# A band of eight heads, whole weight rows, earlier state-model loads and a new order in a two-branch attention and state-space kernel

## The chip, the cores and the metric

The kernel runs on one core of a Trainium2 chip. TensorE does the matrix products into PSUM, VectorE (DVE), ScalarE (ACT) and GpSimd (POOL) work on SBUF and, but for GpSimd, on PSUM; SyncE (SP) issues nearly all DMAs. Each engine takes its instructions in order and waits on semaphores. The metric is the device time of one execution in microseconds. Three runs of the kernel before gave a median of 142.18 us (141.98 to 142.41).

## What is computed

Two branches read 2,048 tokens of width 448 each, in bf16; their outputs stand side by side in an output of 2,048 x 896.

```python
# A: attention, H = 16 heads of Dh = 28, window W = 8 with a dilation of 2
qkv = x @ wqkv                       # 448 x 1344
idx = pos[:, None] - arange(8) * 2   # a token sees itself and 7 earlier ones, two apart
logits = einsum("bhsd,bhswd->bhsw", q, kg) * Dh**-0.5   # masked where idx < 0
o = einsum("bhsw,bhswd->bhsd", softmax(logits), vg)
a = o.reshape(B, S, D) @ wo
# B: a diagonal complex state model with 448 states
h = Lam_bar * h + Bu[:, t, :]        # over 2,048 steps
y = 2.0 * einsum("blp,dp->bld", hseq, Cmat).real + x * Dskip
```

## The kernel before

One function defines some 60 small steps (`@op`), and a string, `ORDER` (L31 to L59), lists 556 calls of them. A loop at the end (L808) runs through the list and emits each step's instructions, so the list sets the order on every engine. A token is a step's name, its indices, after `@` the PSUM banks that it uses, and for an eviction from PSUM the engine: `.` is ScalarE, `=` VectorE. Capital names (`QK`, `AV`, `C`) are mostly TensorE steps, the small ones (`qk`, `av`, `c`) their evictions. The loads that stand ahead of the list (L138 to L162) are issued first.

Branch A. x is loaded token-major into `xbuf`; its first 1,024 tokens are transposed on TensorE (`XA`, `XH`, evicted by `xa`, `xh`), the second 1,024 by four DMA transposes into `xT` (L157). `wqkv` is loaded by `w_load` (rows 0 to 383, as three tiles of 128) and `w_half` (the last 64 rows, twice, into the lower and the upper partitions); before the change the columns of q and k come in pieces of 256 and 192. GpSimd copies the last 64 columns of q and k together into `wq6` (L211). `QS` and `QK` make q and k, head dimension on partitions (`part`, L231), `V_` makes v token-major, also through L231. `P` multiplies q by eight shifted k on VectorE (L346), `E_` sums over each head's 28 rows by a matmul with a 0/1 matrix (L358, L362), four column tiles of 32 side by side. `lt`, `TR`, `tr` scale and transpose the logits, `sma`, `smb`, `smc` are the softmax, into `attn`, for a token 8 weights by 16 heads.

The weighted sum over a token's window is a banded matrix product, and the band is built by DMA. `AL` shifts the weights to the key's token by a matmul with a shifted identity (L426, L429) and `al` evicts them into a row of zeros, `Ak`: for one key token and one tile of tokens, 128 weights (8 places by 16 heads) and then zeros up to 640. `ad` writes the rows to a DRAM buffer `pd`; `sp` reads it back with a row pitch that is 16 elements short (L444, four DMAs per call, 32 partitions each), so that each key token's weights land 16 elements further right than the one's before: `PT` holds, for every key token (partition), the weights of 135 query tokens, 16 heads side by side. `AV` (L470, L475) multiplies v of a head (32 columns) by this band; the moving operand takes every 16th element, `4 * hg + hh:H * n:H`. One call has 16 such matmuls, in four groups of four heads, each head in its own 32 columns of the array; calls with B = 1 have four more of 7 columns. There are eight calls for each half of the tokens (B = 0, B = 1), two of a tile pair's four head groups and two parities. `av` evicts, `W_` multiplies by `wo` (L488), `w` evicts and `ow` stores.

Branch B. x is loaded a second time, regrouped, into `xnB` (`LX`, twelve DMAs, L616) and transposed by four DMAs into `xbuf` (`xt`, L644); `Bn` (L162) is transposed into `BT` (`BD`, L620), C into `Cw` (`CD`). `BU` is the input product (L231), `BR`, `UP`, `DN`, `H_` are rotations that carry the state within four steps and between halves, `sa`, `sb`, `sd` the scan on VectorE, `cs` and `ca` scale C, `C` is the output product (L755), `c` adds x times Dskip (`xd`) and `oc` stores.

SP takes its DMAs in the order of the program text and of the list: the loads, `BD`, `xt`, `LC`, `XR`, `CD`, `wo`, then `ad` and `sp`, then the stores.

Of the kernel before, what the change touches and what calls it, by code (L numbers as in the profile page):

```python
# [9 lines left out]
BF16 = mybir.dt.bfloat16  # L10
# [11 lines left out]
PW = H * (128 + 7)  # L22
# [9 lines left out]
WU@0 XA00@0 XA01@1 xa00= XH0@2 xa01. PP@3 xh0. pcopy pa QS00@4 pb pd_ pc XH1@5 XA11@6 pe xh1. XA10@7 ty0 QS10@0  # L32
xa11. xa10= qk000. QK061@13 tf0 qk010. QK021@25 QS01@6 ty5 P000 ts00 QK041@74 QS11@0 tf5 QK040 pf P001 qk001. QK060
qk011. pg ts10 ts05 qk041. QK020 ts20 ts15 qk040. V_100@60 P010 qh001. ty1 qk021. V_010@47 rb1 ts25 qh000. tf1 V_011
qk020. V_101 QK031@51 qh011. rb0 QK030 v100. ty2 P011 v101. QK050@26 LX qk031. tf2 qk030. ts01 V_001@01 P020 QK051
ts11 V_000 qk050. qk051. P021 qh010. V_110@52 v011. rb3 ts21 QK140@63 v000. P030 ty4 v010. ts02 QK120@70 v001. tf4
hc0 rb2 ts12 V_111 ts04 QK141 E_00@41 v110. v111. E_01 P031 qk141. E_02 qk140. QK101@52 QK121 ts22 P040 QK100 qk120.
qk121. P041 ts14 BD V_510@36 ty3 ts24 qk100. P050 V_511 ty6 V_501@70 V_500 v511. tf6 P051 xt0 QK110@56 ts06 ts16
v510. tf3 v500. QK111 E_03 P060 qk110. E_04 v501. E_05 xt2 qk101. P061 V_410@37 ts03 ts13 P100 qk111. E_06 ts26 ts23
V_411 P101 QK131@50 lt00 QK161@26 xt3 QK130 lt01 v410. P110 v411. TR0@4 qk131. P111 QK150@13 qk130. tr0. xt1 P120  # L40
V_401@70 QK151 QK160 qk151. P121 qk150. E_10@54 P130 qh110. LC E_11 qh101. V_400 qh100. P131 qh111. E_12 sma0 v401.
E_13 hc1 v400. XR BU301@31 BU401@26 BU001@07 BU400 P140 smb0 P141 BU300 P150 OZ z40. BU000 z30. ci1= ci2. BR31 ci3=
BR41 CD1 BU200@23 z00. P151 z31. ci0. BR01 P160 CD3 BU310@01 z41. z01. P161 BU311 CD2 BU501@67 BU201 E_14 smc0 E_15
CD0 E_16 BR32 lt11 BU500 lt10 z20. TR1@4 z32. BR21 z50. BU100@52 tr1= z21. sma1 BR51 BU211@06 z51. BU101 BU210 z10.
OP pm3 xd2 smb1 pm0 wo BR11 BU011@43 z11. smc1 BU111@75 BR22 BU010 z22. ca3 AL0@2 BR23 BR02 al0. BR33 BU110 pm1 z02.
ad0 z23. xd1 z33. ca1 BR03 BR12 AL1@0 cs3 BU410@24 al1= z12. xd3 z03. ad1 BR13 UP3 sp0 UP0 pm4 z13. BU411 cs1 y0.
BU601@07 UP1 y3. BR42 UP2 y1. BU600 ca2 sa0 pm2 AL2@3 z42. sp1 BU510@15 z60. sb0 y2. ca6 BU511 BU611@20 sd0 BR43
BR52 BR61 z43. BU610 al2. z61. cs2 ad2 z52. DN1@6 AL3@3 dn1 BR53 DN0@7 al3. UP4 H_21@1 dn0 BR62 z53. H_11@6 h21 ad3
y4. H_01@3 z62. H_10@7 h11 UP5 H_20@4 H_00@1 y5. BR63 h20 ca4 AV030@2 sp2 sa2 AV020@6 AV010@5 av030. AV031@4 av020.
cs4 AV000@2 av010. AV021@6 av031. sb2 AV011@5 av000. AV001@4 av011. cs6 W_30@2 av021. sp3 h01 av001. W_10@5 sd2 z63.  # L50
w30. W_20@6 w10. ow30 ca5 UP6 W_00@3 w20= ow10 h10 W_31@4 ow20 y6. w00. DN3@2 DN2@5 W_11@6 ca0 dn2 ow00 dn3 W_21@7
sa4 W_01@0 w11. w21. ow11 H_12@3 H_22@5 w01. w31= ow21 H_13@2 AV121@6 sb4 ow01 ow31 AV110@7 av121. AV120@0 h12 h13
AV100@4 av120. sd4 AV131@6 av110. av100. AV130@3 av131. AV101@2 av130. sa6 AV111@0 av101. DN4@7 h22 DN5@4 av111.
W_70@6 dn4 W_40@3 dn5 w70. cs5 H_02@2 ow70 W_50@0 sb6 h00 W_61@5 w50. sd6 w40. H_14@7 ow50 W_71@4 w61. ow40 cs0
H_03@6 ow61 W_51@1 h03 W_60@0 w51. w71. DN6@3 W_41@5 dn6 ow71 h14 H_15@6 H_26@1 w41. w60= H_25@4 H_24@3 ow41 H_23@7
h25 C32@5 ow60 h23 ow51 h26 H_04@0 H_05@4 h24 C31@7 xd0 C33@1 h05 h15 C23@3 c33 c32 oc33 H_06@4 oc32 C30@6 c23 h06
oc23 H_16@1 C20@5 h16 h04 C22@3 c31 oc31 C21@4 c22 c30 oc22 h02 C12@1 oc30 c20 C11@0 oc20 c12 c21 oc12 C13@7 oc21
c11 oc11 C03@3 C10@6 c03 c13 oc03 C02@2 oc13 C01@5 c02 c10 oc02 C00@1 oc10 c01 oc01 c00 oc00
# [3 lines left out]
def kernel(  # L62
# [64 lines left out]
    def w_load(c, n, *at):  # L127

        for d in at:
            SP.dma_start(wq[:, 0:3, c + d:c + d + n], wq_r[:, :, c + d:c + d + n])  # L130

    def w_half(s, c, n, *at):

        o, i = (bass.AP(t.tensor, t.offset + c + at[0], [list(t.ap[0]), [D, len(at)], [1, n]])
                for t in (wq[64 * s:64 * s + 64, 3], A_wqkv[384:448]))
        SP.dma_start(o, i)  # L136
# [3 lines left out]
    w_load(0, 256, 0, D)  # L140
    w_half(0, 0, 256, 0, D)
    SP.dma_start(xnA[:, 4:8], xA_r[:, 4:8])
    w_half(1, 0, 256, 0, D)
    w_load(256, 192, 0, D)
    for s in range(2):
        w_half(s, 256, 192, 0, D)
    w_load(0, D, 2 * D)
    for s in range(2):
        w_half(s, 0, D, 2 * D)

    xA1 = xbuf[:, 8 * D:].rearrange("p (t n) -> p t n", n=2 * D)
    for d0, d1, b, c in ((0, D, 8, 0), (D, 512, 12, 384), (512, 896, 12, 0)):
        SP.dma_start(xA1[:, :, d0:d1], xA_r[:, b:b + 4, c:c + d1 - d0])

# [5 lines left out]
    for ri, b in enumerate((B_B_re, B_B_im)):  # L160
        for d0, d1, c in ((0, D, 0), (D, 512, 384)):
            SP.dma_start(Bn[64 * ri:64 * ri + 64, :, d0:d1], b[:, c:D].rearrange("(g p) d -> p g d", p=64))  # L162


    xnB = keep.tile([128, 4, T, D], BF16, tag="xnB")
    xP = xnB.rearrange("p c j d -> p c (j d)").rearrange("p c (a n) -> p c a n", a=2)
    xB_r = B_x[0].rearrange("(q p h a b) d -> h p q a b d", q=2, p=128, h=2, a=2)
# [249 lines left out]
    @op  # L417
    def AL(g):
        p = pp["al", g] = ps()
        p4 = p.rearrange("p (t w h) -> p t w h", t=4, w=W)  # L420

        def at(t0, n, cc):
            return attn[:, t0:t0 + n, cc:cc + H]
        for w in range(W):
            cc = 32 * (3 - w // 2) + 16 * (w % 2)
            PE.matmul(p4[:, :, w, :], shf[:, 135 + w:263 + w], at(4 * g, 4, cc), start=(w == 0), stop=True, skip_group_check=True)  # L426
            if w > 0:
                n = 4 if g < 3 else 2
                PE.matmul(p4[:, 0:n, w, :], shf[:, 7 + w:135 + w], at(4 * g + 2, n, cc), start=False, stop=True,  # L429
                          skip_group_check=True)  # L430

    @op
    def al(g, e):
        evict(e, late["Ak"][g].rearrange("p (s n) -> p s n", n=640)[:, :, 0:128], pp.pop(("al", g)).rearrange("p (s n) -> p s n", n=128))
# [5 lines left out]
    @op  # L440
    def sp(g):
        sl = (4 * g) % NS
        for s in range(4):
            SP.dma_start(late["PT"][32 * s:32 * s + 32, sl:sl + 4, 512 * s:512 * s + 624],  # L444
                         pd_ap(g, 32 * s * 2560, [[2560 - H, 32], [640, 4], [1, 624]]))
# [17 lines left out]
    @op  # L463
    def AV(B, hg, par):
        PT = late["PT"]
        p = pp["av", B, hg, par] = ps()
        if B > 0:
            for hh in range(4):
                PE.matmul(p[32 * hh:32 * hh + 32, 0:7], v_s[:, 8 * B - 2 + par, 4 * hg + hh, :],
                          PT[:, 6 + par, 128 * H + 4 * hg + hh:PW:H], start=True, stop=True, skip_group_check=True)  # L470
        for bl in range(4):
            t = 8 * B + 2 * bl + par
            n = 135 if bl < 3 else 128
            for hh in range(4):
                PE.matmul(p[32 * hh:32 * hh + 32, 128 * bl:128 * bl + n], v_s[:, t, 4 * hg + hh, :],  # L475
                          PT[:, t % NS, 4 * hg + hh:H * n:H], start=(bl == 0 and B == 0), stop=True, skip_group_check=True)
# [133 lines left out]

    @op
    def LX():
        for hh in range(2):
            for d0, d1, b, c in ((0, D, 0, 0), (D, 512, 1, 384), (512, 896, 1, 0)):
                for q in range(2):
                    SP.dma_start(xP[:, 2 * hh + q, :, d0:d1], xB_r[hh, :, q, :, b, c:c + d1 - d0])  # L616
# [164 lines left out]
    @op  # L781
    def OP():
        cl.close()
        s6 = pool("a_pt")
        for n, shape in (("oT", (2, 4, 2, 512)), ("PT", (NS, PW)), ("wo", (4, D)), ("ya", (6, D))):
            late[n] = s6.tile([128, *shape], BF16, tag=n, name=n)

        late["Ak"] = [Ak0[:, 0], Ak0[:, 1], late["oT"][:, 1].rearrange("p a b n -> p (a b n)")[:, 0:2560],
                      late["ya"].rearrange("p k n -> p (k n)")[:, 0:2560]]
        late["n"] = 0  # L790

    @op
    def pm(i):
# [3 lines left out]
        elif i == 3:  # L797
            POOL.memset(late["wo"].rearrange("p a n -> p (a n)").bitcast(F32), 0.0)
        else:
            POOL.memset(late["PT"][:, 4 * i:4 * i + 4].rearrange("p t n -> p (t n)").bitcast(F32), 0.0)  # L800
# [42 lines left out]
```

## Time and profile before

| what | us |
|---|---|
| median of three runs | 142.18 |
| the profiled execution | 141.91 |
| its span, first to last instruction | 140.2 |
| TensorE busy | 133.6 |
| VectorE busy | 111.7 |
| ScalarE busy | 91.4 |
| GpSimd busy | 22.7 |

The costliest TensorE groups are L231 (input products of both branches), L755, L475, L488 and L358. In a group's row the numbers after the bar are the busy time in us, the mean length of one instruction in ns, and the idle time of the engine before them. Matmuls are pipelined: one that lasts 421 ns does not keep the next from starting, so what one costs is read from the chain or from the distance between starts, not from its length. A row of the chain has its start, its length and its work; a window has its bounds and length, the busy time of each engine, the granted clock, the DMA engines' share and what they moved in GB/s.

### The profile page before, as it was taken

The page shows a single profiled execution, that of the slowest core. Times are in us where ns is not written, and L with a number is a line of the kernel's source. Part 1 is how long each engine was busy: PE and PEld are TensorE (multiplying, and loading weights), DVE is VectorE, ACT ScalarE, POOL GpSimd, SP SyncE. Part 2 cuts the span into 40 slices and gives each one's busy share as a digit, 9 for nine tenths or more (in the row PEclk, how much of TensorE's full clock was granted, in tenths as well). Part 3 has the DMA queues.
Part 4 walks back from the last instruction along what each step waited for, and adds up shares of the span by engine and source line. Part 5 has one row for each costly group of instructions (what it writes and reads, how often), then busy time and mean ns, then how long its engine had stood idle before and what let it go on. Part 6 is the DMA issues. An engine that isn't in the chain of part 4 may idle for free.

```text
span 140.2 us, 2881 instructions
## 1 busy us (share of the span) xinstructions
PE 133.6 (95%) x1074; PEld 64.0 (46%) x1083; DVE 111.7 (80%) x201; ACT 91.4 (65%) x186; POOL 22.7 (16%) x39
## 2 busy tenths in 40 slices
PE   6988999999999999999999999999999999999990
PEld 6742443433434334343455445554554555555540
DVE  0178999999899999988998989628975889777351
ACT  4279999999999899467999996599274430000000
POOL 6709000000000000049995000000000000000000
PEclk9999999999999999999999999999999999999999
DMA  4999389999999989981049996183400421214232
GB/s 126 246 267 245 91 164 189 190 312 221 165 224 209 222 184 351 271 191 34 0 188 308 227 379 167 38 202 111 133 7 0 131 81 54 98 33 153 73 101 65
DMA packets 38116, 22.62 MB, mean 161 GB/s; under 512 B 22935, under 2 KB 37079, under 8 KB 38103
## 3 DMA queue, kind: packets, MB, share of 16 engines
q1 hardware_dynamic: 38040, 22.45, 64.2%
q8 instruction: 8, 0.13, 0.4%
q14 instruction: 5, 0.04, 0.1%
q10 hardware_dynamic: 63, 0.01, 0.0%
HBM read 11.68 MB, written 6.29 MB: 128 GB/s over the span
## 4 chain that ended last, share of the span: by engine, by line
PE 89%; SPq 4%; DMA 3%; issue 1%; POOL 0%; DVE 0%; POOLq 0%
PE ps L231 38%; PE ps L755 15%; PE ps L475 11%; PE ps L488 9%; PE ps L358 4%; PE ps L670 3%; PE ps L736 3%; DMA wq<-in_A_wqkv_dram 3%; SPq L130 1%; SPq L136 1%; PE ps L315 1%; PE ps L362 1%; PE ps L426 1%; PE ps L376 1%; PE ps L723 1%
## 5 line engine op out<-in xcount | busy, mean ns | idle before, releaser
L346 DVE TENSOR_TENSOR pr<-qf,kf 128x2048 bf16<-128x2048 bf16 x24 | 28.2, 1218 | 0.3 <-ACT kf L112 0.3
L231 PE MATMUL ps<-xbuf,BT 128*128 128x512 bf16 (+1 forms) x110 | 23.9, 380 | 0.4 <-issue 0.3
L755 PE MATMUL ps<-Cw,Z 128*128 128x448 bf16 x112 | 21.8, 352 | 0.0
L231 PE MATMUL ps<-xT,wq 128*128 128x512 bf16 (+1 forms) x92 | 20.8, 380 | 0.9 <-POOL wq L211 0.5
L112 ACT CAST Z<-ps 128x512 bf16<-128x512 f32 (+1 forms) x35 | 16.1, 513 | 1.6 <-PE ps L670 1.2
L475 PE MATMUL ps<-PT,v_s 128*32 128x135 bf16 (+1 forms) x256 | 16.0, 419 | 0.0
L755 PEld LDWEIGHTS <-Z 128*128 128x128 bf16 x112 | 10.9, 98 | 10.4
L231 PEld LDWEIGHTS <-BT 128*128 128x128 bf16 (+1 forms) x112 | 8.8, 97 | 12.2 <-issue 3.4
L761 DVE TENSOR_TENSOR xbuf<-ps,xnB 128x448 bf16<-128x448 f32 x16 | 9.5, 620 | 6.0 <-PE ps L755 5.9
L741 DVE TENSOR_TENSOR Z<-ps,Z 128x512 bf16<-128x512 f32 x21 | 13.6, 680 | 0.7 <-PE ps L736 0.7
L112 ACT CAST oT<-ps 128x512 bf16<-128x512 f32 x17 | 9.6, 587 | 7.0 <-PE ps L475 7.0
L488 PE MATMUL ps<-wo,oT 128*128 128x448 bf16 x64 | 13.3, 353 | 0.0
L231 PEld LDWEIGHTS <-wq 128*128 128x128 bf16 (+1 forms) x96 | 7.7, 97 | 10.9 <-issue 2.5
L231 PE MATMUL ps<-wq,xT 128*128 128x448 bf16 (+1 forms) x64 | 12.5, 355 | 0.0
L800 POOL MEMSET PT<- 128x4320 f32 x3 | 11.0, 3699 | 2.0 <-ACT Z L112 2.0
L475 PEld LDWEIGHTS <-v_s 128*32 128x32 bf16 x256 | 7.4, 113 | 6.3 <-issue 0.4
L112 ACT CAST ya<-ps 128x448 bf16<-128x448 f32 (+1 forms) x14 | 7.0, 540 | 4.1 <-PE ps L488 1.9
L632 ACT ACTIVATE ctmp<-Cw,c2t 64x448 f32<-64x448 bf16 x14 | 9.3, 667 | 0.3
L488 PEld LDWEIGHTS <-oT 128*128 128x128 bf16 x64 | 6.2, 98 | 5.7 <-ACT oT L112 0.5
L231 PEld LDWEIGHTS <-xT 128*128 128x128 bf16 (+1 forms) x64 | 5.0, 97 | 7.8 <-issue 4.0
L112 ACT CAST v_s<-ps 128x448 bf16<-128x448 f32 x16 | 8.2, 533 | 0.1
L112 ACT CAST qf<-ps 128x512 bf16<-128x512 f32 x12 | 6.9, 595 | 0.0
(146 smaller groups left out, 184.7 us busy)
## 6 DMA issues: line engine op xcount, KB each, us to landing
PT<-pd SPq DMA_DIRECT2D x16, 156.0 KB, 3.5
xnB<-in_B_x_dram SPq DMA_DIRECT2D x2, 896.0 KB
out_dram<-ya SPq DMA_DIRECT2D x16, 112.0 KB, 1.9
out_dram<-xbuf SPq DMA_DIRECT2D x16, 112.0 KB, 1.7
pd<-Ak SPq DMA_DIRECT2D x2, 640.0 KB, 3.4
xbuf<-in_A_x_dram SPq DMA_DIRECT2D x2, 448.0 KB
xnB<-in_B_x_dram SPq DMA_DIRECT2D x4, 224.0 KB, 5.6
xnB<-in_B_x_dram SPq DMA_DIRECT2D x4, 192.0 KB, 4.0
```

What stands on the lines that cost most here:

```text
L112: (ACT.copy if e == "A" else V.tensor_copy)(o, i)
L231: PE.matmul(o, l, r, start=(first and i == 0), stop=(not first and i == len(pairs) - 1 and not more[s]))
L346: V.tensor_tensor(t[:], q.unsqueeze(1).to_broadcast((128, 4, 512)), k4, ALU.mult)
L358: PE.matmul(acc[s][32 * i:32 * i + 32], E[:, f, ws, :], t[:, i, :], start=(f == 0 and ws == 0), stop=False)
L475: PE.matmul(p[32 * hh:32 * hh + 32, 128 * bl:128 * bl + n], v_s[:, t, 4 * hg + hh, :], PT[:, t % NS, 4 * hg + hh:H * n:H], start=(bl == 0 ...
L488: PE.matmul(p[:, 0:D], late["oT"][:, b // 4, hg, par, 128 * (b % 4):128 * (b % 4) + 128], late["wo"][:, hg, :], start=(hg == 0), stop=(hg ...
L632: ACT.activation(t[a:a + 64, 0:D], Cw[b:b + 64, g, :], ACTF.Copy, scale=c2t[a:a + 64, g:g + 1])
L670: PE.matmul(pp["z", g, j][:], rot(g, 0), late["Z"][:, g, j - 1, :], start=False, stop=True)
L741: V.tensor_tensor(zz, pp.pop(("h", j, g))[:], zz, ALU.add)
L755: PE.matmul(p[:, 0:D], z, Cw[:, g, :], start=(g == 0), stop=(g == G - 1))
L761: V.tensor_tensor(yo, pp.pop(("c", j, ct))[:, 0:D], xnB[:, ct, j, :], ALU.add)
L800: POOL.memset(late["PT"][:, 4 * i:4 * i + 4].rearrange("p t n -> p (t n)").bitcast(F32), 0.0)
```

## The change

Four things change.

1. The band holds eight heads side by side (`HS = 8`) in two groups, not 16 in one. `AL` writes its places in runs of 8, `al` evicts eight pieces of 64 instead of four of 128, a row of `Ak` has eight pieces of 320 with 64 weights each, `sp` reads with a pitch 8 short, runs of 312 elements (624 bytes) instead of 624 elements, twice as many, and `AV` takes every 8th element. Sizes in bytes stay.
2. The q and k columns of `wqkv` are loaded as one piece of 896 columns.
3. The first six of the twelve loads of `xnB` are issued ahead of the four transposes of x, the other six after `Bn`, whose four loads are issued in another order; the step `LX` is gone.
4. The list is ordered anew. It has the same steps but `LX`. The evictions `xa00`, `ci3`, `al1`, `w20`, `w31` and `w60` go from VectorE to ScalarE, `xa01`, `xh0` and `w51` the other way.

```diff
+HS = 8
-PW = H * (128 + 7)
+PW = HS * (128 + 7)
...
-WU@0 XA00@0 XA01@1 xa00= XH0@2 xa01. PP@3 xh0. pcopy pa QS00@4 pb pd_ pc XH1@5 XA11@6 pe xh1. XA10@7 ty0 QS10@0
-xa11. xa10= qk000. QK061@13 tf0 qk010. QK021@25 QS01@6 ty5 P000 ts00 QK041@74 QS11@0 tf5 QK040 pf P001 qk001. QK060
...
+WU@0 XA00@0 XA01@1 xa00. PP@2 XH0@3 pcopy xa01= pa xh0= pb QS10@4 pd_ pc pe XA11@5 ty0 XA10@6 qk010. XH1@7 xa11.
+xa10= QS00@2 xh1. tf0 ty5 V_011@01 QK021@34 qk000. QS11@5 tf5 pf P000 QS01@6 QK041@72 QK020 P001 ts00 qk011. ts05 pg
...
+z62. H_00@5 H_01@0 ca4 H_21@3 h00 H_11@7 BR63 h21 AV011@4 h11 AV000@5 al3. sa2 AV031@3 av011. ad3 z63. AV020@7 sp2
+av000. AV001@1 y5. av020. AV010@4 sb2 av001. AV030@5 av010. AV021@6 cs4 av030. H_20@7 av031. UP6 sd2 sp3 H_10@1
+W_20@4 y6. W_10@5 w20. av021. h20 W_30@3 ow20 ca0 DN2@2 W_21@4 dn2 sa4 DN3@6 W_11@7 w21. w10. H_22@2 ow21 w30.
+W_00@4 dn3 ca5 ow30 h10 W_01@5 cs0 W_31@3 w00. cs5 w01. H_13@6 ow00 H_02@1 sb4 w31. AV100@4 ow01 w11. ow31 AV110@5
+av100. ow11 sd4 AV131@3 ow10 av110. AV121@7 av131. AV101@4 sa6 AV111@5 av101. h22 AV130@3 av121. h13 av111. AV120@4
+av130. sb6 H_03@2 av120. DN4@7 W_41@5 dn4 sd6 W_60@6 w41. H_23@3 ow41 H_14@4 w60. W_50@7 h23 ow60 h03 DN5@5 W_71@6
...
-    w_load(0, 256, 0, D)
-    w_half(0, 0, 256, 0, D)
+    w_load(0, 2 * D)
+    w_half(0, 0, 2 * D)
     SP.dma_start(xnA[:, 4:8], xA_r[:, 4:8])
-    w_half(1, 0, 256, 0, D)
-    w_load(256, 192, 0, D)
+    w_half(1, 0, 2 * D)
+    w_load(2 * D, D)
     for s in range(2):
-        w_half(s, 256, 192, 0, D)
-    w_load(0, D, 2 * D)
-    for s in range(2):
-        w_half(s, 0, D, 2 * D)
+        w_half(s, 2 * D, D)
...
+    def x_load(hh):
+        for d0, d1, b, c in ((0, D, 0, 0), (D, 512, 1, 384), (512, 896, 1, 0)):
+            for q in range(2):
+                SP.dma_start(xP[:, 2 * hh + q, :, d0:d1], xB_r[hh, :, q, :, b, c:c + d1 - d0])
+
+    x_load(0)
+
     xT = s2.tile([128, 2, 7, 512], BF16, tag="xT")
     for t in range(4):
         SP.dma_start(xT[:, 1, :, 128 * t:128 * t + 128], xA1[:, t], transpose=True)
...
-    for ri, b in enumerate((B_B_re, B_B_im)):
-        for d0, d1, c in ((0, D, 0), (D, 512, 384)):
+    for d0, d1, c in ((0, D, 0), (D, 512, 384)):
+        for ri, b in enumerate((B_B_re, B_B_im)):
             SP.dma_start(Bn[64 * ri:64 * ri + 64, :, d0:d1], b[:, c:D].rearrange("(g p) d -> p g d", p=64))
+    x_load(1)
...
-        p4 = p.rearrange("p (t w h) -> p t w h", t=4, w=W)
+        p4 = p.rearrange("p (t g w h) -> p t g w h", t=4, g=H // HS, w=W)
...
-            SP.dma_start(late["PT"][32 * s:32 * s + 32, sl:sl + 4, 512 * s:512 * s + 624],
-                         pd_ap(g, 32 * s * 2560, [[2560 - H, 32], [640, 4], [1, 624]]))
+            SP.dma_start(late["PT"][32 * s:32 * s + 32, sl:sl + 4, :, 32 * HS * s:32 * HS * s + 39 * HS].rearrange("p t g n -> p (t g) n"),
+                         pd_ap(g, 32 * s * 2560, [[2560 - HS, 32], [40 * HS, 64 // HS], [1, 39 * HS]]))
...
                 PE.matmul(p[32 * hh:32 * hh + 32, 128 * bl:128 * bl + n], v_s[:, t, 4 * hg + hh, :],
-                          PT[:, t % NS, 4 * hg + hh:H * n:H], start=(bl == 0 and B == 0), stop=True, skip_group_check=True)
+                          PT[:, t % NS, (4 * hg + hh) // HS, (4 * hg + hh) % HS:HS * n:HS], start=(bl == 0 and B == 0), stop=True, skip_group_check=True)
```

## The prediction

> **What bounds the kernel now.** I read the page's busy shares first, then the chain of waits, then the groups by form, and last the windows and the timeline around the places that the diff touches.
>
> ```profile
> PE 133.6 (95%) x1074; PEld 64.0 (46%) x1083; DVE 111.7 (80%) x201; ACT 91.4 (65%) x186; POOL 22.7 (16%) x39
> PE 89%; SPq 4%; DMA 3%; issue 1%; POOL 0%; DVE 0%; POOLq 0%
> ```
>
> TensorE is the bound, and the granted clock is 0.999, so no throttle hides in it. The chain in order of time enters TensorE at 11.25 us and leaves it at 136.66 us for one last addition; between, "issue" is a few times 0.05 to 0.16 us. A gain must therefore be less streaming time on TensorE, or a shorter start.
>
> ```profile
> 46.90 0.98 PE ps L358 x16
> 83.30 7.85 PE ps L475 x124
> 101.41 0.97 PE ps L475 x14
> ```
>
> These chain pieces carry the forecast. L358 (the logit sums) and L475 (attention times values, AV) both put four matmuls of 32 columns side by side in the array. Sixteen L358 matmuls stream 512 columns each in 0.98 us: 0.245 us per group of four, 0.48 ns per column. Sixteen L475 matmuls stream only 135 (or 128) columns and take the same: 7.85 us for eight operations, 0.245 us per group, 1.81 ns per column. The visible difference is the moving operand: L358 reads neighbours (2 bytes apart), L475 reads every 16th element of the band (32 bytes apart).
>
> ```profile
> L475 PE MATMUL ps<-PT,v_s 128*32 128x135 bf16 x192 | 14.7, 421 | 0.0
> L358 PE MATMUL ps<-pr,E 128*32 128x512 bf16 x96 | 6.1, 381 | 0.0
> 83.20:106.30 23.10, 23.10 (x328) 11.99 (x327) 16.74 (x36) 15.85 (x29) 0.00 (x0) 1.00 0.40 115
> ```
>
> A single L475 matmul lasts longer than an L358 one with a quarter of its columns. The last line is the window of both AV phases (length, then busy time of PE, PEld, DVE, ACT, POOL, clock, DMA share, GB/s): TensorE 23.1 of 23.1 us, VectorE 16.7, ScalarE 15.9. Those two limit what a faster AV can give.
>
> The start, from the timeline and two windows:
>
> ```profile
> 6.91 0.82 PE L315 MATMUL ps<-xT,wq 128*128 128x512 bf16 x2
> 8.55 0.41 PE L284 MATMUL ps<-ident,xbuf 128*64 128x128 bf16 x4 [0.50 <-DMA xbuf<-in_A_x_dram]
> 11.25 0.39 PE L231 MATMUL ps<-xT,wq 64*128 64x512 bf16 x2 [0.55 <-POOL wq L211]
> ...
> 4.20:6.50 2.30, 2.15 (x24) 1.75 (x22) 0.69 (x1) 0.44 (x1) 1.97 (x7) 1.00 0.86 225
> 53.00:57.00 4.00, 4.00 (x20) 1.82 (x19) 4.00 (x6) 3.90 (x8) 0.00 (x0) 1.00 1.07 381
> ```
>
> TensorE waits 0.5 us for x and 0.55 us for GpSimd's copy of the weights. Weights in 512-byte runs arrive at 225 GB/s; rows of 3,584 bytes later at 381.
>
> **The change part by part.** The profiled execution took 141.91 us (span 140.2 and 1.7 around it); the median of the three runs is 142.18, 0.27 more, added at the end.
>
> *Band of eight heads.* AV reads every 8th element, 16 bytes apart, half the step. No row shows that step. Ends: no change (1.81 ns), and L358's 0.48 ns, which makes a group 0.065 us and over 64 groups (16 operations by 4) saves 11.5 us. A loss I exclude for this part: the matmul covers half the bytes. A straight line between the two rows gives 1.10 ns, 0.149 us a group, 6.2 us saved; a time in proportion to the step gives 0.123 us and 7.8 us saved. I take 7.0, nearer to the 32-byte row than to the neighbours' row.
>
> The Trainium skill, SBUF — State Buffer, Specifications (TRN2), speaks against this: SBUF lines are 16 bytes, and full bandwidth needs at least two accesses per line. At 16 bytes, as at 32, every element opens its own line, so by that rule the step saves nothing and the time is the second case below; the trace agrees that 32 bytes are slow (1.81 against 0.48 ns) and shows no step of 16.
>
> What is late next: both AV phases, with the W, H and DN steps between, are 23.2 us of TensorE in the new order and would be 16.2. Counted from the new list by the rows, VectorE has there five h (0.68), four sa or sd of 1.69, one sa of 1.16, scans of 1.35, 1.35 and 0.68, three cs (0.675) and two dn (0.42): 17.6 us by single durations, 16.3 with the overlap that the page shows (111.7 busy where the single durations sum to 120). ScalarE has fifteen av (0.587), eight w (0.54), two ca and four more: 17.5, or 15.8 back to back (three oT evictions took 1.58 us). So the stretch ends with these engines, not TensorE: 16.3 plus about 0.9 of handing over, 17.2, since the early W steps need all four of their av, which queue on ScalarE behind al3 and z63. Saved: 23.2 - 17.2 = 6.0 us. Bounds: 6.9 (stretch 16.3) and 4.0 (stretch 19.2).
>
> AL has the same matmuls in runs of 8; its 15 take 0.43 us, 29 ns each, as short as any group here, so zero, and at most 60 x 27 = 1.6 us if each took a transpose's 56 ns. The al eviction keeps its elements: zero (v_s in runs of 28 takes 0.533 us for 448, Z in runs of 512 takes 0.600 for 512). Zeroing covers the same bytes. The band's reload keeps its bytes, with runs of 624 instead of 1,248: four DMAs per sp, issue 0.43 us against 0.47 for a 256-run x load, so 0.2 per sp on SP. At 76 to 80 us the bus moved 227 GB/s in 1,248-byte runs, 512-byte runs made 225: zero, and a rival below. The first AV comes 0.3 us sooner after AL1 in the new list (10.9 against 11.2 by the rows); sp1's last issue ended at 78.1 and the longest landing is 4.6, so at 82.7 at the latest against 83.2: slack 0.5 covers it; +0.1.
>
> *Whole rows of wqkv.* QS10 waits for 803 KB (896 columns of 448 rows) behind the first x tiles (used from 4.59), instead of 458 KB. At 225 GB/s from 4.2 that is 7.8 us; at 381, 6.3. TensorE is free at 6.9. The next x tiles (459 KB at 299 GB/s, the rate of 6.5 to 8.5 us) follow at 7.8 to 9.3, then 1.02 us of transposes and QS00 0.97: 10.0 (both before and QS10 done at 7.9) to 11.3, with the V weights there by 11.5. The kernel before has the same steps done at 11.25. So -1.2 to +0.2, middle -0.5; VectorE and ScalarE are busy 37.2 and 37.6 of the next 38.7 us, so I keep -0.2. GpSimd's copy waits for two of these loads as before, but QK060, its first reader, now comes some 7 us of TensorE work after V_011: that wait (0.55 us, inside the 11.25 above) goes.
>
> *x ahead of the transposes.* Six issues (0.47 to 0.8 us) move in front of the four transposes on SP, where SP waited 4.2 us for x: issue hidden. Their 917 KB are not: at 256 to 381 GB/s, 2.4 to 3.6 us on the bus ahead of the transposes, whose last was issued at 19.4 and landed 3.1 later, at 22.5: now 24.9 to 26.1. Their first reader, QK121, is 14.4 us of TensorE work after V_011 (10.9 to 11.5), at 25.3 to 25.9: a wait of 0 to 0.8 us. I take +0.1, because the x that they transpose also comes sooner. BD (5.13 us of issue) and xt behind it move 3 us forward: nothing, BU starts at 50. Bn's halves change places: nothing.
>
> *Order and engines.* Six evictions go from VectorE to ScalarE, three back (0.6 us each): hidden, VectorE is the closer of the two to TensorE.
>
> **Sum**: 141.91 - 6.0 - 0.2 + 0.1 + 0.1 = 135.9, and with the 0.27: **136.2 us**. Its own range: 134.6 (stretch 16.3, start -1.0) to 138.4 (stretch 19.2).
>
> **The rivals.** *The step does not matter* (AV stays at 0.98 us per operation). For it: each element is fetched alone at either step, and four streams at 1.81 ns are one fetch per 0.45 ns, near the 0.48 ns per column of a full stream, as if one element per cycle were shared by four. Against: L358's four streams do not share. Then 142.18 - 0.2 + 0.2 = 142.2, from 141.2 (start -1.0) to 143.6 (start +0.2, transposes +0.8, first AV +0.4). More of it lies above than below: the start's gain is shared with two busy engines, the waits are not.
>
> *The band's DMAs go by runs, not bytes* (the other side). Place: AV011, which needs sp0 and sp1, eight DMAs of 160 KB, 0.70 us each at 227 GB/s. If twice the runs take twice the time: 8 x 0.70 = 5.6 us late, less the slack of 0.2: 5.4. Without an AV gain that gives 147.6, at half the price 144.9. It decides as soon as the delay passes what AV saves (6.0), or the slack where AV saves nothing. Against: 225 GB/s in 512-byte runs.
>
> *Half a gain*: 1.4 ns per column saves 0.056 x 64 = 3.6 us, below the other engines' limit: 138.6.
>
> **How the numbers follow.** Forecast 0.45; half a gain 0.05; step without effect 0.38 (faster 0.06, same 0.10, slower 0.22); by runs 0.12, all slower. Faster 0.56, same 0.10, slower 0.34, where 0.3% (0.43 us) is about what can be told from no change here. The range for 8 in 10 takes the forecast's low end and the second case's high end: 134.6 to 143.6.
>
> **What would show it.** Eight AV of the first phase in 4 to 5 us instead of 7.85, L475 near 300 ns each, VectorE or ScalarE above 90% from the first AV to the last, W steps waiting for oT. If the step does nothing: L475 stays at 420 ns. If runs count: idle before the first L475, released by PT. At the start: QS10 at 6.9 to 7.8, QS00 done by 11.3. A PE wait for xT near 25 us would make the x load wrong. The prediction is wrong above all if the read step is not what slows L475.

## The result and the profile after

The changed kernel takes 144.47 us (median, 144.31 to 144.57) against 142.08 beside it: ratio 1.0164, 95% interval 1.0143 to 1.0185. It is 2.4 us slower; 136.2 was predicted. Its profiled execution took 144.46 us, span 142.7. Some comparisons below state a ratio rather than two medians, because an execution whose clock was disturbed is left out of the ratio.

The page of the changed kernel: busy shares, the granted clock in 40 slices, the chain by engine.

```profile
PE 135.0 (95%) x1083; PEld 65.2 (46%) x1083; DVE 110.3 (77%) x198; ACT 93.9 (66%) x189; POOL 22.7 (16%) x39
PEclk9965999999999999999999999999999999999997
PE 90%; DMA 5%; SPq 1%; DVE 0%; issue 0%
```

TensorE is still the bound, with 1.4 us more to do than before, not less. One digit row is new: the clock falls in the third and fourth slice. And DMA holds 5% of the chain where it held 3%.

The chain in order of time, the two groups that the forecast rested on, and the window of both AV phases:

```profile
2.99 7.60 DMA xbuf<-in_A_x_dram
10.63 1.46 PE ps L272 x12
...
85.22 7.75 PE ps L478 x122
```

```profile
L478 PE MATMUL ps<-PT,v_s 128*32 128x135 bf16 x192 | 14.8, 417 | 0.0
L360 PE MATMUL ps<-pr,E 128*32 128x512 bf16 x96 | 6.1, 381 | 0.0
85.20:108.60 23.40, 23.40 (x330) 13.05 (x330) 17.07 (x36) 16.93 (x34) 0.00 (x0) 1.00 0.51 139
```

L478 is the old L475. With half the step it takes the same: eight AV in 7.75 us (7.85 before), 417 ns each (421). The window of both phases is full of TensorE, 23.4 of 23.4 us. So the whole term that the forecast was made of, 6.0 us, is missing, and on top of that something costs 2.4 us. That is at the start (timeline of TensorE, then windows of all engines):

```profile
8.30 1.46 PE L317 MATMUL ps<-xT,wq 128*128 128x512 bf16 x3 [2.26 <-DMA wq<-in_A_wqkv_dram]
10.63 1.46 PE L272 MATMUL ps<-ident,xbuf 128*128 128x128 bf16 x12 [0.33 <-DMA xbuf<-in_A_x_dram]
```

```profile
8.30:10.60 2.30, 2.00 (x4) 0.38 (x4) 0.07 (x1) 0.27 (x1) 0.00 (x0) 0.50 1.12 274
10.60:12.60 2.00, 1.97 (x17) 1.61 (x17) 0.47 (x1) 0.90 (x2) 1.37 (x2) 0.50 1.14 283
17.30:50.00 32.70, 32.70 (x225) 13.90 (x223) 31.55 (x52) 32.28 (x72) 0.00 (x0) 1.00 1.09 199
```

The first product of q and k (QS10, L317) starts at 8.30 us, after 2.26 us of waiting for the weights; the kernel before started its own at 6.91. The second half of x, behind the weights on the bus, is transposed from 10.63 (8.55 before). The same three matmuls that took 0.82 us take 1.46: the granted clock is 0.50 from 7.97 to 14.80 us. From 17.3 to 50 us TensorE then does not pause once (in the kernel before it pauses 0.26 us there).

So two questions were open. Why did half the read step save nothing? And how do late weights, which cost 1.4 to 2.1 us on the timeline, come to 2.4 us at the end?

### The profile page after: what moved, and what is told of

It is laid out like the page before. It is cut to its first block, busy times and chain, and to the rows that moved or that the text cites. A ratio compares the mean times of both kernels' runs of the same rounds, so it can differ in the third digit from the quotient of the medians.

```text
span 142.7 us, 2875 instructions
## 1 busy us (share of the span) xinstructions
PE 135.0 (95%) x1083; PEld 65.2 (46%) x1083; DVE 110.3 (77%) x198; ACT 93.9 (66%) x189; POOL 22.7 (16%) x39
## 4 chain that ended last, share of the span: by engine, by line
PE 90%; DMA 5%; SPq 1%; DVE 0%; issue 0%
PE ps L233 37%; PE ps L751 15%; PE ps L478 11%; PE ps L491 8%; DMA xbuf<-in_A_x_dram 5%; PE ps L360 4%; PE ps L666 3%; PE ps L732 3%; PE ps L317 2%; PE ps L272 1%; PE ps L318 1%; PE ps L364 1%; PE ps L428 1%; PE ps L378 1%; PE ps L678 1%; PE ps L719 1%
## 5 line engine op out<-in xcount | busy, mean ns | idle before, releaser
L348 DVE TENSOR_TENSOR pr<-qf,kf 128x2048 bf16<-128x2048 bf16 x24 | 28.0, 1220 | 0.4 <-ACT kf L113 0.4
L113 ACT CAST Z<-ps 128x512 bf16<-128x512 f32 (+1 forms) x35 | 16.4, 509 | 3.3 <-PE ps L666 1.3
L478 PE MATMUL ps<-PT,v_s 128*32 128x135 bf16 (+1 forms) x256 | 15.9, 415 | 0.0
L113 ACT CAST ya<-ps 128x448 bf16<-128x448 f32 (+1 forms) x16 | 8.0, 541 | 5.7 <-PE ps L491 4.4
L478 PEld LDWEIGHTS <-v_s 128*32 128x32 bf16 x256 | 8.2, 113 | 5.4 <-issue 0.4
L113 ACT CAST kf<-ps 128x512 bf16<-128x512 f32 x12 | 6.9, 605 | 2.5 <-PE ps L318 2.5
```

What stands on the lines that cost most here:

```text
L113: (ACT.copy if e == "A" else V.tensor_copy)(o, i)
L348: V.tensor_tensor(t[:], q.unsqueeze(1).to_broadcast((128, 4, 512)), k4, ALU.mult)
```

## Experiments: which part loses

**The band alone undone**: the changed kernel with 16 heads side by side.

```diff
-HS = 8
+HS = 16
```

> The changed kernel with 16 heads side by side again, all else as changed. Theory A (the loss sits at the start: late weights, and the half clock that follows TensorE's idle time): 144.3 to 144.6 us, eight AV of the first half in 7.8 us, first product still near 8.3 us. Rival B (the band of eight costs something, in its reload or in AL): 142 to 143.5 us. Rival C (the read step of 16 bytes did help a little and hides a larger loss): slower than 144.6, AV operations at 0.98 instead of 0.97 us.

Measured 145.29 us, ratio 1.0215 (1.0153 to 1.0278), above every range expected but rival C's. The interval overlaps that of the changed kernel, and in its profiled execution the first product started 0.8 us later (9.06 us), which the band has no part in. What is the band's is in the chain:

```profile
86.69 7.86 PE ps L478 x120
```

7.86 us for eight AV at a step of 32 bytes, 7.75 at 16: the band of eight gains 0.1 us there, as rival C had it, but the larger loss is not its own, as the next run shows.

**The weight rows alone undone**: the changed kernel with the loads of before, pieces of 256 and 192 columns.

```diff
-    w_load(0, 2 * D)
-    w_half(0, 0, 2 * D)
+    w_load(0, 256, 0, D)
+    w_half(0, 0, 256, 0, D)
```

> The changed kernel with wqkv loaded in the pieces of before (256 and 192 columns), all else as changed. Theory A: the first product of the weights starts at 6 to 6.6 us instead of 8.3, the granted clock stays at 1.0 in the first 15 us, and the time falls by 1.8 to 2.6 us to about 142.2. Rival B or the order as cause: no more than 0.5 us less, because the work behind the start is the same.

Ratio 1.0036 (0.9994 to 1.0077), profiled execution 141.9 us, span 140.2: the kernel before, as far as can be told. QS10 starts at 6.42:

```profile
6.42 0.81 PE L324 MATMUL ps<-xT,wq 128*128 128x512 bf16 x2 [0.25 <-ACT xT L113]
PEclk9999999999999999999999999999999999999999
```

It waits for a transposed x, not for weights, and the clock stays whole. Not in every execution, though: five kept the whole clock and took 141.9 to 142.5 us, and three at a mean granted clock of 0.983 to 0.988 took 143.5 to 143.8, which widens the interval; where their clock fell was not traced. So the weight rows carry most of the loss: 1.8 us by the two ratios, 2.5 by the spans of the profiled executions. Band, order and the earlier x together cost at most 1.1 us by the interval, and nothing in the profiled execution.

**The weight rows alone done**: the kernel before with the opposite edit and nothing else.

```diff
-    w_load(0, 256, 0, D)
-    w_half(0, 0, 256, 0, D)
+    w_load(0, 2 * D)
+    w_half(0, 0, 2 * D)
```

> The kernel before with wqkv in whole rows, its order, band and x loads as they were. Theory A: its first product of the weights moves from 6.9 to 8.0 to 8.5 us, the clock falls to half for some us, and it takes 143.5 to 145 us. If whole rows cost only with the new order: within 0.5 us of 142.1.

Measured 145.68 us, ratio 1.0248 (1.0195 to 1.0302), more than the 143.5 to 145 expected. QS00, the first product in that order, waits 1.60 us for wqkv and starts at 8.25, and the clock is halved from 9.4 us. So the rows alone cost 3.5 us in the old order. That this order suffers more than the new one is not shown: the run with 16 heads, which has the new order and whole rows and was made on the same chip, lost 3.1.

## Experiments: how the late start reaches the end

The first guess was the half clock.

**Clock kept up**: the changed kernel with 40 matmuls of zeros ahead of QS10.

```diff
+    @op
+    def WV():
+        p = ps()
+        for _ in range(40):
+            PE.matmul(p[:, 0:128], wz[:], wz[:], start=True, stop=True)
...
-WU@0 XA00@0 XA01@1 xa00. PP@2 XH0@3 pcopy xa01= pa xh0= pb QS10@4 pd_ pc pe XA11@5 ty0 XA10@6 qk010. XH1@7 xa11.
+WU@0 XA00@0 XA01@1 xa00. PP@2 XH0@3 pcopy xa01= pa xh0= pb WV@5 QS10@4 pd_ pc pe XA11@5 ty0 XA10@6 qk010. XH1@7 xa11.
```

> The changed kernel with 40 more matmuls of zeros (some 2.2 us) in TensorE's wait for the weights, which adds no wait and brings no data sooner. If the half clock is most of the loss: granted clock 1.0 from 8.3 to 15 us, first product at 8.3 as before, time 142.3 to 143.0 us. If the waiting itself is the loss and the clock little: 144.0 to 144.5 us.

Measured 144.77 us, 1.0173 (1.0106 to 1.0239). The clock was 1.0 throughout, and no gain shows. To be sure, both kernels were run once more, on one chip.

> The changed kernel unaltered, beside the others on the same chip: 144.3 to 145.3 us, first product of the weights at 8.3 to 9.1 us, first eightfold product on VectorE at 16 to 17 us.

> The changed kernel with 40 matmuls of zeros in TensorE's wait, again, now beside the unaltered one. If the half clock carries the loss: 1.5 to 2 us below the unaltered kernel. If what counts is that VectorE and ScalarE, busy for 97% of the next 35 us, start late by as much as the weights do: within 0.5 us of it, though the granted clock is 1.0 all through the start.

144.75 and 144.56 us: 0.2 us, less than the uncertainty. Mending the half clock alone gives nothing that shows. But the traces show a second limit. VectorE and GpSimd, the changed kernel and then the one with the zeros:

```profile
12.74 2.31 DVE L593 TENSOR_SCALAR kM<-iot,fT 128x256 f32<-128x256 f32 x1
15.62 0.35 DVE L593 TENSOR_SCALAR kM<-iot,fT 128x256 f32<-128x256 f32 x1
12.67 2.23 POOL L217 MEMSET Ak<- 128x2560 f32 x1
```

```profile
11.76 2.82 DVE L599 TENSOR_SCALAR kM<-iot,fT 128x256 f32<-128x256 f32 x1
12.20 2.23 POOL L217 MEMSET Ak<- 128x2560 f32 x1
```

The same instruction takes 0.35 us alone; beside GpSimd's fills it lasts until the fill of the band's rows is over: it ends at 15.05 and 14.58, 0.15 us after that fill in both (in the second it had started during the smaller fill of v_s, 11.31 to 12.26). The products of q and k (L348, two bf16 tensors) queue behind it: in the kernel before the first started at 11.80; after the change at 16.41. The products themselves are not held: in the version with the old weight pieces the fills ran from 11.21 to 12.30 and from 12.24 to 14.47 us, and two products took the same 1.2 us each as elsewhere:

```profile
11.86 2.36 DVE L355 TENSOR_TENSOR pr<-qf,kf 128x2048 bf16<-128x2048 bf16 x2
```

In the run with the zeros the chain that ended last leaves TensorE for this held operation, where that of the changed kernel stays on TensorE:

```profile
11.84 2.75 DVE kM L599
15.95 2.35 DVE pr L354 x2
```

The Trainium skill, SBUF — State Buffer, SBUF: two separate sides, gives the rule: VectorE in a two-port mode and GpSimd take a shared pair of ports as an exclusive lock for a whole instruction, and an operation with two SBUF inputs collides only with a GpSimd operation that reads SBUF. The trace agrees on both counts: the single-input TENSOR_SCALAR was held 2.0 and 2.5 us, the two-input product was not.

**Fills moved**: GpSimd's two fills (L215, L217) ahead of its copy of the weights, into its idle time from 6.4 us; four kernels on one chip.

```diff
+    v_s = vpool.tile([128, NT, H, 32], BF16, tag="v_s")
+    POOL.memset(v_s[:, :, :, DH:32], 0.0)
+    Ak0 = smp.tile([128, 2, 2560], BF16, tag="Ak0")
+    POOL.memset(Ak0.rearrange("p k n -> p (k n)").bitcast(F32), 0.0)
     wq6 = s2.tile([128, 4, 2, 64], BF16, tag="wq6")
     POOL.tensor_copy(wq6[:], wq[:, :, 0:2 * D].rearrange("p k (a n) -> p k a n", a=2)[:, :, :, 384:D])
-    v_s = vpool.tile([128, NT, H, 32], BF16, tag="v_s")
-    POOL.memset(v_s[:, :, :, DH:32], 0.0)
-    Ak0 = smp.tile([128, 2, 2560], BF16, tag="Ak0")
-    POOL.memset(Ak0.rearrange("p k n -> p (k n)").bitcast(F32), 0.0)
```

> The changed kernel with GpSimd's two fills (v_s, 0.95 us, and Ak, 2.23 us) issued ahead of its copy of the weights, so that they run in the idle 6.4 to 11.2 us. In the changed kernel the first phase on VectorE, a TENSOR_SCALAR of 128x256 that takes 0.35 us elsewhere, ran from 12.74 to 15.05 us, and the fill of Ak from 12.67 to 14.90. Theory A (late data brings that operation into the fill, which holds it; VectorE and ScalarE are the clock of the stage up to 50 us): the operation takes 0.35 us, the first product of q and k starts near 14.4 us rather than 16.41, and of these 2.0 us between half and all reach the end: 142.5 to 143.7 against 144.5. Theory B (only the late weights and x matter, the collision is covered by other work): 144.3 to 144.8, wherever the product starts. The small operations on VectorE at 6.4 to 8.4 us, which run beside the fills now, may be held up to 2 us; nothing needs them before 10 us.

144.33 us, 1.016 (1.012 to 1.020): theory A of that expectation falls. The operation takes 0.34 us and the first product starts at 15.04, 1.4 us sooner, and what of this reaches the end is less than the uncertainty.

In the kernel before, the same move is as idle:

> The kernel before with the two fills moved ahead. There the second phase on VectorE took 1.46 us instead of 0.35 (12.94 to 14.40, the fill 12.02 to 14.25), behind the first product. Theory A as far as it goes here: 1.1 us earlier second product, 141.2 to 142.2. Theory B: 141.9 to 142.4. Were the fills to hold the small operations at 7 to 9 us, and these the first phase at 10.4: up to 1 us slower, 142.4 to 143.

142.37 us, 1.0011 (0.9994 to 1.0027).

What both edits left out is TensorE's own account. The window from 17 us to the end (bounds and length, then busy time of PE, PEld, DVE, ACT, POOL, clock, DMA share, GB/s), for the kernel before, the changed one (with its first 17 us and then a second execution on the chip of the zeros), with zeros, with fills moved, and with both:

```profile
17.00:146.00 129.00, 118.91 (x970) 55.38 (x976) 102.14 (x169) 80.17 (x160) 14.16 (x7) 0.99 0.61 150
```

```profile
0.00:17.00 17.00, 13.20 (x92) 7.46 (x93) 7.51 (x24) 8.28 (x19) 8.56 (x32) 0.80 0.92 243
17.00:146.00 129.00, 121.84 (x993) 57.72 (x993) 102.74 (x175) 85.64 (x171) 14.16 (x7) 0.99 0.61 143
17.00:146.00 129.00, 121.25 (x986) 57.79 (x993) 102.69 (x175) 85.79 (x171) 14.16 (x7) 0.99 0.61 144
```

```profile
17.00:146.00 129.00, 119.75 (x975) 56.74 (x981) 102.26 (x175) 84.06 (x167) 14.16 (x7) 0.99 0.63 144
PE ps L233 <- ACT v_s L113: 0.8, 2, 0.6
```

```profile
17.00:146.00 129.00, 121.59 (x991) 57.36 (x990) 101.49 (x174) 85.41 (x170) 14.15 (x7) 1.00 0.62 144
```

```profile
17.00:146.00 129.00, 120.79 (x987) 57.97 (x984) 100.66 (x169) 84.65 (x168) 14.16 (x7) 0.99 0.63 145
```

What TensorE still has to do at 17.0 us, plus what it idles from there (span less 17.0 less that work), is the rest of the kernel:

| kernel | TensorE work left at 17.0 us | idle from there | span |
|---|---|---|---|
| before | 118.9 | 4.3 | 140.2 |
| changed | 121.8 | 3.9 | 142.7 |
| changed, on the chip of the zeros | 121.3 | 4.5 | 142.8 |
| zeros (full clock) | 119.8 | 5.7 | 142.4 |
| fills moved | 121.6 | 3.8 | 142.4 |
| zeros and fills moved | 120.8 | 4.0 | 141.8 |

The two executions of the changed kernel differ by 0.5 to 0.6 us, so the table is good to about that. The changed kernel leaves 2.3 to 2.9 us more of TensorE's work for later, and has no idle time to make it up. The zeros take 1.5 to 2.1 of them back and lose 1.1 to 1.8 again to idle time; 0.8 of it is TensorE waiting for ScalarE's v, as ScalarE and VectorE are behind. Moving the fills brings those two forward, but the clock still halved there, for 3.4 us, and TensorE is the later one, so that helps nobody. The reading is of two limits, each hiding behind the other; the last row is the test.

**Both at once**: the two edits above together.

> The changed kernel with both edits at once: 40 matmuls of zeros ahead of the first product of q, and GpSimd's two fills ahead of its copy of the weights. Each alone gave 0.0 to 0.3 us of the 2.4 lost. Theory C (two limits, either of which is enough: at the half clock TensorE leaves 121.6 to 121.8 us of its work for after 17.0 us, against 118.9 in the kernel before; at the full clock it leaves 119.8, but then waits 1.3 us in 17.3 to 50 for ScalarE and VectorE, which the fill made late): with both mended TensorE leaves 119.5 to 120 us of work and waits as little as in the kernel before, about 4.3 us behind 17.0, so the span is 141.0 to 141.3 and the time 142.7 to 143.1. Theory D (the late weights and x cost what they cost, whatever the clock and the fill do): 144.2 to 144.6, as with either edit alone.

Measured 143.51 us (143.32 to 143.71), 1.0076 (1.0058 to 1.0094): an interval that does not meet that of either edit alone, and 1.2 us better than the changed kernel by the ratios. So the two did hide each other. But it is about half the loss and falls between the ranges of theory C, which had 1.4 to 1.8 us, and theory D: 120.8 us of work were left, not 119.5 to 120. In this execution the x tiles could be transposed only from 11.06 us (10.27 in the run with zeros alone), so the data was later there; how much of the other half, some 1.1 us, is the late weights and how much the late x was not separated.

## Experiments: which step would help

If each element of the band opens a 16-byte line of its own at a step of 32 and of 16 bytes, the first step that can gain is 8. So the version with the old weight pieces was run with four and with two heads side by side.

```diff
-HS = 8
+HS = 4
```

> The changed kernel with the weights in pieces and four heads side by side: AV reads 8 bytes apart, and the band's reload goes in runs of 312 bytes. Theory D (a column costs one fetch of 16 bytes for each of the four streams, whatever the step, until two elements share such a piece): group of four from 0.243 to about 0.12 us, eight AV of the first half in 4 to 5 us, and with a stretch limited by VectorE and ScalarE 136.5 to 139 us unless the reload delays the first AV. Rival E (the four matmuls do not run side by side at all because they bring other weights, and the step never mattered): 7.8 us again and 142 us or, with a slower reload, more.

> As the run with four, but two heads side by side: AV reads 4 bytes apart, the reload goes in runs of 156 bytes, eight times the number of before. Theory D: group of four at 0.07 to 0.12 us, AV operations bound by their 16 issues, some 0.5 us. Rival E: 0.243 us again. In both, if the reload goes by runs, TensorE waits for PT ahead of the first AV, by several us, and the total is 143 us or more; if it goes by bytes, it does not wait.

137.1 us, ratio 0.9621 (0.9582 to 0.9661), and ratio 0.9811 (0.9774 to 0.9848). Four heads, by form, with the chain piece and the wait; then two heads:

```profile
L485 PE MATMUL ps<-PT,v_s 128*32 128x135 bf16 x192 | 8.4, 299 | 0.9 <-DMA PT<-pd 0.8
85.24 3.86 PE ps L485 x114
PT<-pd SPq DMA_DIRECT2D x16, 156.0 KB, 4.7
```

```profile
L485 PE MATMUL ps<-PT,v_s 128*32 128x135 bf16 x192 | 7.1, 283 | 4.5 <-DMA PT<-pd 4.5
101.23 0.45 PE ps L485 x11
PE ps L485 <- DMA PT<-pd: 4.5, 2, 2.7
```

Eight AV fall from 7.76 to 3.86 us, one of the second phase from 0.97 to 0.49. At 4 bytes an AV of the second phase takes 0.45, but at half the clock; at the full clock, ahead of its fall at 87.18 us, 25 matmuls start between 86.62 and 87.00, a group of four every 0.062 us:

```profile
86.62 0.59 PE L485 MATMUL ps<-PT,v_s 128*32 128x135 bf16 x25 [2.68 <-DMA PT<-pd]
86.70:87.00 0.30, 0.30 (x25) 0.30 (x28) 0.30 (x1) 0.03 (x1) 0.00 (x0) 1.00 1.01 410
102.00:103.00 1.00, 1.00 (x56) 0.99 (x51) 1.00 (x3) 1.00 (x3) 0.00 (x0) 0.50 0.72 235
```

Per group of four heads, at the full clock: 0.245 us at 32 bytes, 0.242 at 16, 0.121 at 8, 0.062 at 4. If a group's 4 x 135 elements are fetched one after the other at 32 and 16 bytes, each fetch is 0.45 ns; at 8 bytes two elements come with one fetch, and 270 fetches of 0.45 ns are 0.121 us; at 4 bytes four do, and 135 fetches are 0.061. The sum fits all four steps. That the four streams take turns at the fetches is argued from this fit: four streams side by side, each with 1.8 ns per fetch, would give the same times. At 4 bytes the time is also about what 135 columns take in a full stream (0.065 at 0.48 ns each), so which of the two bounds there cannot be told. In the first phase of the version with four heads the weight loads are busy 3.67 of 3.90 us:

```profile
85.20:89.10 3.90, 3.86 (x121) 3.67 (x122) 3.77 (x8) 3.59 (x9) 0.00 (x0) 1.00 0.71 233
```

They are not what holds it at 0.121 us, since with two heads they keep pace with 0.062. The Trainium skill's rule that the prediction weighed (SBUF — State Buffer, Specifications (TRN2): 16-byte lines, two hits per line for full bandwidth) agrees in part: no gain from 32 to 16 bytes, half the time at 8. But at 8 bytes, with two hits per line, a column still took twice the time that it took at 4; here, with four matmuls side by side, the full pace came with four.

The shorter runs have a price: the band's reload lands after 3.6 us in runs of 624 bytes, 4.7 in runs of 312, and AV waits 0.8 us for it; with runs of 156 bytes 4.5 us, and the clock halves twice behind these waits. That is the rival "by runs", which at 624 bytes did not happen.

The gain is 4.7 us of span (140.2 to 135.5), and AV saves 7.7 (16 times 0.48). The stretch from the first AV to the last goes from 23.3 us to 16.4, 6.9 less, and it starts at 85.2 us instead of 83.0, of which 0.8 is the wait for the band. Most of the rest is the start of this execution: there the fill held the VectorE operation for 2.89 us, and the first product of q and k started at 15.24 instead of 11.86; with the fills moved, below, the first AV starts at 84.03.

Is the new order needed for the gain? The kernel before with four heads and nothing else, the band's lines as in the change:

```diff
+HS = 4
-PW = H * (128 + 7)
+PW = HS * (128 + 7)
```

> The kernel before with the band of four heads alone: old weight pieces, old order, old place of x. If the read step of 8 bytes is the gain: the eight AV from 83 us on take 3.9 us (7.8 before), the later eight 0.49 each (0.97), in sum 7.7 us of TensorE, less what the first AV waits for the band, which comes in runs of 312 bytes: 136 to 138. If the new order and x ahead of the transposes were what made room for it: 139 to 142.

137.31 us, 0.9656 (0.9620 to 0.9693): no. And the two fills moved as well, with the new order and with the old:

> The version with before's weight pieces and a band of four heads, with the same two fills moved ahead. Its profiled execution had the same collision (the operation took 2.89 us, the first product started at 15.24). Theory A: the first product starts near 12.3 to 12.8 us and the time falls by 1 to 2.5 us from 136.9, to 134.5 to 136. Theory B: 136.4 to 137.3. The first AV still waits for the band (0.8 us), which limits what an earlier start gives unless the band starts earlier too.

> The kernel before with the band of four heads and the fills moved ahead. The band alone gave 137.3 there; the fills alone gave nothing (142.4), as TensorE is the bound behind 17 us. Theory C: nothing where TensorE is the bound, but the band of four makes the first AV wait 0.5 us for the band, which comes off VectorE and ScalarE; so 0 to 0.8 us from there: 136.5 to 137.4. In the version with before's pieces and the new order the fills went with 1.0 us less (137.1 and 136.1 on two chips): if that was theirs, 136.0 to 136.6.

136.12 us, 0.9579 (0.9553 to 0.9605), and 137.11, 0.9634 (0.9614 to 0.9653). With the old order the fills are worth no more than their uncertainty, and with the new one the interval also meets that without them (0.9582 to 0.9661). The version with the new order, old weight pieces, four heads and early fills is the fastest seen, 6.2 us below the kernel before; that it beats the old order by half a per cent rests on two chips, each against its own runs of before, and its intervals do not meet.

## Why the prediction was wrong, by its own steps

**Read step (7.0 us of TensorE, 6.0 realised).** This is the step that failed: it saved 0.1 us in the first phase. The prediction took a value between a straight line from 1.81 ns at 32 bytes to 0.48 ns for neighbours and a time in proportion to the step. The relation has a corner: flat down to 16 bytes, then halved at 8 and again at 4. The prediction had named the right case as a rival (142.2 us, chance 0.38, "one fetch per 0.45 ns") and noted the rule that speaks for it; the argument it held against that, that L358's four streams do not share, does not hold if eight neighbours come with one fetch: 4 x 512 elements are then 256 fetches of 0.45 ns, 0.115 us, and hide in the 0.245 that 512 columns take anyway. The limit put on a faster AV, 17.2 us by VectorE and ScalarE, did not bind where AV was faster: with four heads the stretch of 16.4 us is full of TensorE (16.1 busy, the next line), and VectorE is busy 14.8.

```profile
85.20:101.60 16.40, 16.12 (x320) 11.49 (x321) 14.77 (x33) 14.48 (x31) 0.00 (x0) 1.00 0.74 184
```

**Whole rows (-0.2, bounds -1.2 to +0.2 us).** Wrong in size and sign: +1.8 to +2.5. QS10 was put at 6.3 to 7.8 us and came at 8.30 (9.1 on another chip), x at 7.8 to 9.3 and came at 10.6, QS00 was to be done by 11.3 and was done at 14.6. The rate was not what failed: from 4.20 to 8.30 us the bus moved 279 GB/s, between the 225 and the 381 that were taken. But that is 1.14 MB, and the sum had only the 0.80 MB of QS10's weights in this time: by 8.3 us the bus had moved 1.68 MB (203 GB/s from the start on), where the first half of x and these weights are 1.26 MB. The other 0.4 MB went to other transfers, by the times of issue perhaps to the second half of x, issued at 2.99 us; which ones they were was not traced. And the bound did not price what a wait of that length does next: 0.50 of the clock for 6.8 us, and VectorE's operation pushed into GpSimd's fill. The idle time of VectorE and ScalarE was taken to limit a gain; it limits a loss only while TensorE has slack, and from 17.3 us it has none. So the rival "the step does not matter" had the AV right and the start wrong: it gave 142.2, reached 143.6 with all its mishaps, and 144.47 was measured. About half of the loss is traced to the clock and the fill together; the other half stays open between late weights and late x. The prediction's own range is also slightly off its terms, which give 134.5 to 138.2 and not 134.6 to 138.4; that changes nothing here.

**x ahead of the transposes (+0.1), order, AL, al and the reload (0 to +0.1).** Right as far as can be told: with the weight pieces of before all of them together are 1.0036 (0.9994 to 1.0077), and the profiled execution has the span of the kernel before. No wait for xT appears, and the reload lands after 3.6 us against 3.5.

## What to carry to other kernels

Read a strided operand by lines, not by bytes: here a smaller step gained nothing until two elements shared 16 bytes, then half. Before a steady time is read as a limit, look at the granted clock beside it. Larger DMA rows were no gain for the first consumer here, which waited for 803 KB instead of 458; split a first load by what is used first. When removing one suspected cause changes nothing, look for a second limit just behind it and remove both before dropping either.

## What the hardware showed that was not expected

The clock fell although TensorE had not been idle for long. In the changed kernel it halved at 7.97 us, and in the 3.41 us up to there TensorE had been busy 1.45:

```profile
4.56:7.97 3.41, 1.45 (x25) 1.19 (x25) 2.22 (x15) 2.22 (x8) 1.67 (x6) 1.00 0.91 288
```

It came back at 14.80, 6.83 us later; with the fills moved it was gone from about 10.4 to 13.8, 3.4 us. The Trainium skill, TensorE: Matmul & The Clock Gate, What's actually happening, counts in free-running windows of 3.41 us and lets an idle one halve the clock. The durations agree, two windows and one, and so do the run's with two heads: down at 87.18 and 100.84 us, back at 90.60 and 104.25, steps of one, three and one window. But the window before the fall was 43% busy, so here less than a whole idle window was enough. In the traces here a window of 1.76 us busy (51%, 5.98 to 9.40 us of the old order with whole rows) still halved the clock, and one of 1.89 us (55%, 7.14 to 10.55 us of the four heads with early fills) did not. Busy time of TensorE is modelled, and where in between the border lies is open.

A GpSimd fill stretched a VectorE operation of 0.35 us to as much as 2.8 us in the rows above, and the profile of the kernel before showed it too, with no idle time to give it away: the seven operations of that form lasted 505 ns in the mean there, 628 after the change, and 347 with zeros and early fills. A mean well above the shortest of its form is the sign.
